# Layers A and B in turn on one core: masks of B built once, four row casts on ScalarE, eight homes for B's first tails

## The chip, the cores and the metric

The kernel runs on one core of one Trainium2 chip. The metric is the device time of one execution in microseconds (us), lower is better. The engines are TensorE (PE, with its weight loads as PEld), VectorE (DVE), ScalarE (ACT), GpSimd (POOL) and SyncE (SP, which here only issues DMAs). ScalarE issues some DMAs as well; its issues are shown as ACTq, those of SyncE as SPq.

## What is computed

Four layers, A, B, A, B, on 2048 rows of 640 numbers, each with a layer norm in front and a residual sum behind:

```python
x = A_x
x = x + _A_ref(_layernorm(x), A_wq, A_wk, A_wv, A_wo, A_beta)
x = x + _B_ref(_layernorm(x), B_mem0, B_Wq, B_Wk, B_Wv, B_Wo, B_seg_len)
x = x + _A_ref(_layernorm(x), ...)
x = x + _B_ref(_layernorm(x), ...)
```

A is attention with 32 heads of 20 over four segments of 512 rows; each segment also reads a running memory `M`, `z` of the segments before it. B is a recurrence over 64 steps of 32 rows; `mem` (8 rows, at first `mem0`) goes in front of each step's rows, and the first 8 rows of a step's result are the next step's `mem`:

```python
for s in range(n_seg):                       # 64 steps
    h = concat([mem, xs])                    # 8 + 32 rows
    q, k, v = h@Wq, h@Wk, h@Wv               # 32 heads of 128
    scores = where(mask, q@k.T * scale, -1e9)
    o = concat_heads(softmax(scores) @ v) @ Wo
    mem = o[:, :M]; outs.append(o[:, M:])
```

`mask` is the same in each step and in both B layers: keys of `mem` are open to everyone, the others are causal.

## The kernel before

`full_kernel` (line 1277) calls `layer_A` (line 217) and `layer_B` (line 728) in turn. B's `Wq` and `Wk` are resident in SBUF; `Wv` and `Wo` share their place with A's tiles and are loaded anew for each B layer. Rows pass from layer to layer through two DRAM tensors, `xres` (float32) and `xres_bf` (bfloat16).

**End of A.** A works through 4 segments by 8 head groups. The last work on a 128-row block is `out_stage_b` (line 330): ten `YP` matmuls in two halves, two DVE sums into `xnew`, a store of `xnew` to `xres` (line 346), a cast to bfloat16 into `xnb` (lines 347 and 348, on GpSimd) and a store of that to `xres_bf` (line 349). `xnb` is in a pool of one buffer, so each cast waits until the store before it has landed. The last segment has four such rows, numbered 0 to 3 here, and they are worked while B begins.

**B's lead-in** (lines 951 to 999) is all that stands ahead of B's first step. In the order in which it is written out:

- `ln_load`, `ln_norm`, `ln_spread` for four blocks of 128 rows: bfloat16 rows in, layer norm (its power on GpSimd), five transposes into a PSUM tile `b_lntps`, and two ScalarE copies, into `HX` and `TX`. `TX` holds the last 8 rows of each step ("tails").
- `init_masks` (line 770, called in line 960): `b_sel` and `b_mask12`, with two DVE sums, two DVE memsets, 16 selects on GpSimd over `b_maskf`, and two DVE casts.
- eight tail units, k = 0 to 7, four with `Wq` and four with `Wk`: 40 matmuls into a PSUM tile `b_tail`, then `tail_evac` (line 906): an evacuation into an SBUF tile `b_tu` (even k on ScalarE, odd k on DVE) and a DMA of 128 KB to DRAM `QKd` (line 913; even k issued by ScalarE, odd k by SyncE). The homes of `b_tu` are the ring `kq` of four buffers for k < 6, and two tiles of the `wk` pool for k = 6 and 7.
- four projections of 512 columns, `b_Kp`, `b_Qp`, `b_Kp`, `b_Qp`, evacuated into `b_kq` tiles of the same ring; then eight loads of `Wo`, 640 KB each (lines 718 and 719, on SyncE).
- transposes `b_TP` of these four, `init_state` (memsets), `tails_load` (line 875), which reads `QKd`.
- eight units `b_vtail` with `Wv`, each evacuated to a tile `b_vt` and stored in two halves to DRAM `VTd` (line 934; odd k issued by ScalarE, even k by SyncE). k = 6 and 7 use again the homes `vt` and `E0` of k = 0 and 1.
- two projections `b_V`, `vtails_in` (line 886), a first tail unit of the next eight steps; then step 0 begins with `b_Ka`.

B's instructions on each engine are kept in written order by a wrapper (line 106 is the wrapper's line, and so stands for most of B; line 135 does the same for A). Across the two layers a scheduler decides the order when the kernel is built. PSUM tiles of the lead-in (`b_lntps`, `b_tail`, `b_Kp`, `b_TP`, `b_vtail` and so on) come from one ring of five buffers. DMAs report by eight completion semaphores that are used in turn, so an issue can also wait for the landing of the DMA eight places before it.

**First A.** On GpSimd it begins with the zeros and pads of its tiles (`P.memset(NM...)`, `pads`) and then turns to `a_EK` and to casts of one element (line 709) that hold back loads of B's resident weights.

Of the kernel before, what the change touches and what calls it, by code (L numbers as in the profile page):

```python
# [18 lines left out]
F32 = mybir.dt.float32  # L19
BF16 = mybir.dt.bfloat16  # L20
ACT = mybir.ActivationFunctionType
ALU = mybir.AluOpType
# [15 lines left out]
def alloc_consts(tc, ctx):  # L38
    cp = ctx.enter_context(tc.tile_pool(name="consts", bufs=1))
    C = Consts()  # L40
    C.pool = cp
    C.identb = cp.tile([128, 128], BF16, name="c_identb")
    C.mhalf = cp.tile([128, 1], F32, name="c_mhalf")
    C.negu = cp.tile([128, 2, 128], BF16, name="c_negu")
    C.bdmask = cp.tile([128, 128], F32, name="c_bd")
    C.pad = cp.tile([128, 2, 12], BF16, name="c_pad")
    W = AWeights()
    W.g = cp.tile([128, 32], F32, name="a_g")
    W.omg = cp.tile([128, 32], F32, name="a_omg")
    return C, W  # L50

# [94 lines left out]
class KeyOrder:  # L146
# [14 lines left out]
    def close(self):  # L161
        for rows in self.rec.values():
            rows.sort(key=lambda r: r[:2])
            for a, b in zip(rows, rows[1:]):
                self.tc.add_manual_dep(b[2], a[2].name, self.info, reason="order")
        self.rec, self.base = {}, None


class AWeights:
# [9 lines left out]

def build_gates(nc, pool, W, A_beta):  # L180
    bb = pool.tile([128, 32], BF16, name="a_beta_bf")
    with nc.allow_non_contiguous_dma(reason="beta bcast"):
        nc.sync.dma_start(bb[:], A_beta.partition_broadcast(128))
    e = pool.tile([128, 32], F32, name="a_beta_e")
    nc.scalar.activation(out=e[:], in_=bb[:], func=ACT.Exp, scale=-1.0)
    nc.vector.tensor_scalar(out=e[:], in0=e[:], scalar1=1.0, scalar2=None, op0=ALU.add)
    nc.vector.reciprocal(out=W.g[:], in_=e[:])
    nc.vector.tensor_scalar(out=W.omg[:], in0=W.g[:], scalar1=-1.0, scalar2=1.0, op0=ALU.mult, op1=ALU.add)

# [27 lines left out]
def layer_A(nc, tc, C, W, x_src, x_dst, src_is_bf16, nseg=4, out_bf16=False, xb_dst=None, load_w=None, side_loads=None):  # L217
    SC = 1.0 / math.sqrt(20.0)
    nc_raw = nc
    nc = _OrdNC(tc, nc_raw, engines=("tensor",))  # L220
    K = KeyOrder(tc, nc_raw, A_LAGS)
# [3 lines left out]
    with ExitStack() as ctx:  # L225
        def pool(name, bufs):
            return ctx.enter_context(tc.tile_pool(name=name, bufs=bufs, reuse_waits="tile"))
# [12 lines left out]
        up = pool("a_unit", 3)  # L240
        wk = pool("a_wk", 2)
# [5 lines left out]
        st = pool("a_state", 1)  # L247
# [17 lines left out]
        def pads(i, eng):  # L265
            for on, dst, k in ((i < 2, Kn, 0), (True, vaug, 1)):
                if on:
                    src = C.pad[:, k, :].unsqueeze(1).unsqueeze(1).to_broadcast([128, 4, 4, 12])
                    (eng.copy if eng is nc.scalar else eng.tensor_copy)(dst[i][:, :, :, 20:32], src)
# [56 lines left out]
        def out_stage_b(n_, tt, halves=(0, 1)):  # L326
            d = SEG[n_]
            oT, xr = d["oT"][tt], d["xr"][tt]
            r0 = n_ * 512 + tt * 128
            if xr is None:  # L330
                xr = wkl.tile([128, D], BF16 if src_is_bf16 else F32, name="a_xr")
                nc.sync.dma_start(xr[:], x_src[r0:r0 + 128, :])
            if n_ == nseg - 1 and (tt or not src_is_bf16):
                d["xnew"] = up.tile([128, D], F32, name="a_xnew", tag="PT") if tt else xr
            elif 0 in halves:
                d["xnew"] = w1l.tile([128, D], F32, name="a_xnew") if src_is_bf16 else xr
            xnew = d["xnew"]
            for half in halves:
                YP = pg.tile([128, 320], F32, name="a_YP", tag="pg")
                for c in range(NCH):  # L340
                    nc.tensor.matmul(YP[:], lhsT=oT[:, c, :], rhs=W.wo[:, c, 320 * half:320 * half + 320],
                                     start=(c == 0), stop=(c == NCH - 1))
                K("xnew").vector.tensor_tensor(out=xnew[:, 320 * half:320 * half + 320], in0=YP[:], in1=xr[:, 320 * half:320 * half + 320], op=ALU.add)
            if 1 not in halves:
                return
            nc.sync.dma_start(x_dst[r0:r0 + 128, :], xnew[:])
            xnb = w1l.tile([128, D], BF16, name="a_xnb")
            K("xnb").gpsimd.tensor_copy(xnb[:], xnew[:])
            nc.sync.dma_start(xb_dst[r0:r0 + 128, :], xnb[:])

        GS = {}
# [220 lines left out]
        P = K("pads").gpsimd  # L572
# [4 lines left out]
                pads(1, P)  # L577
        pads(2, P)
        pads(3, P)
        K.base = None  # L580
        proj_q(0)
        proj_kv(0, 0)
# [67 lines left out]
        for g in range(NGR + 2):  # L650
            n, G = divmod(g, 8)
# [36 lines left out]
        for tt in range(4):  # L688
            out_stage_b(nseg - 1, tt)
# [38 lines left out]
def layer_B(nc, tc, C, W, x_src, xb_src, x_dst, mem0, B_Wv, B_Wo, nsteps=64, out_bf16=False, tag=""):  # L728
    SCB = 1.0 / math.sqrt(128.0)
    nc_raw = nc  # L730
    nc = _OrdNC(tc, nc_raw, engines=ORDER_ENGINES)
# [4 lines left out]
    with ExitStack() as ctx:  # L736
        def pool(name, bufs):
            return ctx.enter_context(tc.tile_pool(name=name, bufs=bufs, reuse_waits="tile"))
# [6 lines left out]
        kqp = pool("b_kqp", 4)  # L745
        W.wo = pool("b_wo", 1).tile([128, 32, D], BF16, name="b_wo")
        st = pool("b_state", 1)
        w2 = pool("b_w2", 2)
        wk = pool("b_wk", 1)
# [11 lines left out]

        Px = st.tile([128, 12, 32], BF16, name="b_Px")
        Pm = st.tile([128, 12, 32], BF16, name="b_Pm")
        mask12 = st.tile([128, 12, 40], BF16, name="b_mask12")
        QZ = [st.tile([128, 16, 24], BF16, name=f"b_QZ{i}") for i in range(2)]
        selm = st.tile([128, 2, 8], BF16, name="b_sel")
        HXz = st.tile([128, NCH, 1, 32], BF16, name="b_HXz")
        OTdef = [wk.tile([128, 32, 32], BF16, name=f"b_OTdef{i}") for i in range(2)]

        def init_masks():  # L770
            nc.vector.tensor_tensor(out=selm[:, 0, :], in0=C.identb[:, 24:32], in1=C.identb[:, 88:96], op=ALU.add)
            nc.vector.tensor_tensor(out=selm[:, 1, :], in0=C.identb[:, 56:64], in1=C.identb[:, 120:128], op=ALU.add)
            negs = wk.tile([128, 32], F32, name="b_negs", tag="PTa")
            nc.vector.memset(negs[:], -1e9)
            maskf = wk.tile([128, 2, 40], F32, name="b_maskf", tag="OTsb")
            nc.vector.memset(maskf[:], 0.0)

            def above(out, rows, ncol, base, chan, colstep=1):
                nc.gpsimd.affine_select(out=out, in_=negs[rows, 0:ncol], pattern=[[colstep, ncol]], compare_op=ALU.is_gt,
                                        fill=0.0, base=base, channel_multiplier=chan)  # L780

            for i in range(4):
                r8, r16, r32 = (slice(32 * i, 32 * i + w_) for w_ in (8, 16, 32))
                above(maskf[r16, 0, 0:8], r16, 8, 8, -1)
                above(maskf[r8, 0, 0:8], r8, 8, 0, -1)
                above(maskf[r32, 1, 8:32], r32, 24, 0, -1)
                above(maskf[r32, 1, 0:8], r32, 8, 24, -1, 0)
            nc.vector.tensor_copy(mask12[:, 0:4, :], maskf[:, 0, :].unsqueeze(1).to_broadcast([128, 4, 40]))
            nc.vector.tensor_copy(mask12[:, 4:12, :], maskf[:, 1, :].unsqueeze(1).to_broadcast([128, 8, 40]))

        def init_state():
            XO_ = bx.tile([64, 320], F32, name="b_XO", tag="XO")
# [9 lines left out]
        HX, TX, QT, KT, VH = {}, {}, {}, {}, {}  # L802
# [103 lines left out]
        def tail_evac(T, k, eng, home=None, dma=nc.sync.dma_start):  # L906
            proj, hg = divmod(k, 4)
            pool_, tg = home or (wk, "tu")
            tu = pool_.tile([128, 8, 8, 8], BF16, name="b_tu", tag=tg)
            evac(eng, tu[:].rearrange("p s h t -> p h s t"), tail_ps[0][:].rearrange("p h (s t) -> p h s t", t=8),  # L910
                 None if proj else SCB)
            o = 256 * proj + 64 * hg
            dma(QKd[8 * T:8 * T + 8, :, o:o + 64].rearrange("s p f -> p s f"), tu[:].rearrange("p s h t -> p s (h t)"))
# [42 lines left out]
        for g in range(n0):  # L956
            ln_norm(g)
            if g < 2:
                ln_spread(ln_ready.pop(0))
        init_masks()  # L960
        nc.gpsimd.memset(HX[0][:, :, 0, 0:8], 0.0)
        with nc.allow_non_contiguous_dma(reason="mem0 transpose load (tiny)"):
            for c in range(NCH):
                nc.sync.dma_start(HX[0][:, c, 1, 0:8], mem0[:, 128 * c:128 * c + 128].rearrange("t p -> p t"))
        for k in range(8):
            tail_unit(0, k, 0, 8, shared=True)
            tail_evac(0, k, "act" if k % 2 == 0 else "dve", (kqp, "kq") if k < 6 else (wk, ("tu", "OTsb")[k - 6]),
                      (nc.sync if k % 2 else nc.scalar).dma_start)
            if k in (1, 3) and ln_ready:
                ln_spread(ln_ready.pop(0))  # L970
# [81 lines left out]
        for s in range(nsteps):  # L1052
# [139 lines left out]
            PTa = wk.tile([128, 2, 4, 40], BF16, name="b_PTa", tag="PTa")  # L1192
# [12 lines left out]
            OTsb = wk.tile([128, 32 * 40], BF16, name="b_OTsb", tag="OTsb")  # L1205
# [161 lines left out]
```

## Time and profile before

| | us |
|---|---|
| three runs | 2710.68, 2709.66, 2705.59 (median 2709.66) |
| the profiled execution | 2707.02 |
| its span, first to last instruction | 2705.3 |
| first A | 0 to about 345 |
| first B: lead-in, then 64 steps | about 345 to 387, then to about 1340 |
| second A | to about 1693 |
| second B: lead-in, then 64 steps | about 1693 to 1736, then to the end |

In a row of a timeline stand the start, the duration, the engine, the line and operation, the tile written and the tiles read, and the count of instructions in the group; in brackets the idle time ahead of it and what ended that. A row with several instructions can have waits inside it. In the chain of waits a row is a start, a duration and the work (or the transfer) that the end waited for; "issue" is time in which the profile shows nothing to wait for. In a table of windows, PEclk is the granted TensorE clock as a share of full speed, and the DMA share is the mean busy share of the 16 DMA engines, which can be a little over 1. "Lead-in 1" and "lead-in 2" are those of the first and the second B; "the end of the lead-in" is the start of step 0's `b_Ka`.

### The profile page before, as it was taken

Reading aid. Unit: us, or ns where it says so; the run is one execution under the profiler, and the core shown is the slowest. Engines: PE = TensorE matmul, PEld = TensorE weight load, DVE = VectorE, ACT = ScalarE, POOL = GpSimd, SP = SyncE. Lnnn points to the kernel's source line nnn. Section 1 sums busy time; section 2 is a strip of 40 time slices with the busy share of each in tenths; the row PEclk is TensorE's granted clock in tenths of the full one; section 3 lists DMA queues with packets and bytes.
Section 4 is the critical chain, followed back from the end, with each engine's and each line's share of the span. In section 5 each row is a group of like instructions: output and inputs, shape, how many; then the busy total and the mean of one; then the engine's idle time right before and its main releaser. Section 6 shows DMA issues by size and latency. Waiting matters only on the chain.

```text
span 2705.3 us, 147013 instructions
## 1 busy us (share of the span) xinstructions
PE 2573.0 (95%) x65480; PEld 1697.2 (63%) x65480; DVE 1694.0 (63%) x4568; ACT 1578.6 (58%) x3712; POOL 717.1 (27%) x1651
## 2 busy tenths in 40 slices
PE   7999989999999999999989998899999999999998
PEld 4566556666666666666655565566666666666666
DVE  8999845555555555555589998355555555555555
ACT  6988935554555555554379888255555555555543
POOL 5677621111111111111146776111111111111110
PEclk9999999999999999999999999999999999999999
DMA  4122451222222222121220114511111121111110
GB/s 154 44 79 79 136 167 39 45 44 42 44 44 44 45 42 45 41 42 28 66 76 21 60 51 134 164 40 40 41 41 43 40 44 40 42 40 40 37 27 20
DMA packets 326620, 156.35 MB, mean 58 GB/s; under 512 B 246241, under 2 KB 310881, under 8 KB 324193
## 3 DMA queue, kind: packets, MB, share of 16 engines
q1 hardware_dynamic: 316384, 145.38, 21.3%
q8 instruction: 512, 8.39, 1.4%
q10 hardware_dynamic: 9600, 1.57, 0.3%
q14 instruction: 124, 1.01, 0.1%
HBM read 95.15 MB, written 51.71 MB: 54 GB/s over the span
## 4 chain that ended last, share of the span: by engine, by line
PE 79%; DVE 11%; ACT 5%; DMA 2%; issue 2%; POOL 1%; SPq 0%; ACTq 0%; DVEq 0%
PE b_OPS L106 11%; PE b_tail L106 6%; DVE a_nm L135 5%; PE b_Ka L106 5%; PE b_Qa L106 5%; PE b_Kb L106 5%; PE b_Qb L106 5%; PE b_Va L106 5%; PE b_Vb L106 5%; PE b_SP L106 4%; PE b_OTP L106 4%; PE b_vtail L106 3%; PE b_PTP L106 3%; PE b_OPSd L106 3%; ACT a_PT L135 3%; PE a_S L106 2%
## 5 line engine op out<-in xcount | busy, mean ns | idle before, releaser
L106 PEld LDWEIGHTS <-b_HX 128*32 128x32 bf16 x15360 | 431.8, 97 | 338.5 <-issue 11.9
L106 POOL TENSOR_TENSOR b_Pm<-b_E,b_rs 128x96 bf16<-128x96 bf16 x128 | 63.4, 496 | 1439.0 <-ACT b_Vth L106 1120.2
L135 DVE TENSOR_REDUCE a_nm<-a_S 128x2 f32<-128x512 f32 (+3 forms) x512 | 394.9, 815 | 30.6 <-PE a_S L106 22.4
L135 ACT ACTIVATE a_PT<-a_T 128x1024 bf16<-128x1024 f32 (+1 forms) x384 | 345.0, 903 | 26.8 <-PE a_T L106 18.2
L106 PE MATMUL b_OPS<-b_wo,b_OTsb 128*32 128x320 bf16 x8192 | 307.3, 300 | 9.7 <-issue 7.7
L106 PEld LDWEIGHTS <-b_OTsb 128*32 128x32 bf16 x8192 | 200.3, 96 | 95.3 <-DVE b_OTsb L106 24.7
L106 DVE CAST b_HX<-b_MT 128x8 bf16<-128x8 f32 x372 | 63.7, 172 | 278.1 <-PE b_MT L106 273.1
L135 POOL TENSOR_SCALAR_AFFINE_SELECT a_PT<-a_PT 128x256 bf16<-128x256 bf16 (+1 forms) x384 | 190.3, 505 | 125.6 <-ACT a_PT L135 124.5
L106 ACT CAST b_msb<-b_OPS 128x64 bf16<-128x64 f32 x378 | 69.4, 256 | 236.8 <-PE b_OPS L106 236.8
L106 ACT CAST b_kq<-b_Kb 128x512 bf16<-128x512 f32 x128 | 74.9, 585 | 202.6 <-PE b_Kb L106 202.6
L106 DVE COPY b_KT<-b_TPak 128x128 bf16<-128x128 bf16 x128 | 28.8, 225 | 226.7 <-PE b_TPak L106 226.7
L106 PEld LDWEIGHTS <-b_kq 128*128 128x128 bf16 x2080 | 117.0, 98 | 75.0 <-ACT b_kq L106 55.7
L106 PE MATMUL b_Ka<-b_wk,b_HX 128*32 128x512 bf16 x2520 | 160.8, 381 | 3.0 <-DVE b_vt L106 3.0
L106 DVE TENSOR_SCALAR b_kq<-b_Qa 128x512 bf16<-128x512 f32 x128 | 88.5, 692 | 116.2 <-PE b_Qa L106 113.3
L106 PE MATMUL b_Va<-b_wv,b_HX 128*32 128x512 bf16 x2520 | 160.8, 380 | 0.0
L106 PE MATMUL b_Qa<-b_wq,b_HX 128*32 128x512 bf16 x2520 | 160.1, 381 | 0.0
L106 PE MATMUL b_Vb<-b_wv,b_HX 128*32 128x512 bf16 x2520 | 160.1, 379 | 0.0
L106 PE MATMUL b_Kb<-b_wk,b_HX 128*32 128x512 bf16 x2520 | 159.2, 379 | 0.0
L106 PE MATMUL b_Qb<-b_wq,b_HX 128*32 128x512 bf16 x2520 | 159.0, 379 | 0.0
L106 DVE CAST b_OTsb<-b_OTP 128x160 bf16<-128x160 f32 (+1 forms) x384 | 122.6, 374 | 39.1 <-PE b_OTP L106 38.9
L106 PE MATMUL b_vtail<-b_wv,b_TX 128*32 128x256 bf16 x2880 | 141.2, 276 | 5.9 <-issue 4.1
L106 ACT ACTIVATE b_E<-b_SP 128x320 bf16<-128x320 f32 (+1 forms) x256 | 81.1, 368 | 109.9 <-PE b_Va L106 97.1
(202 smaller groups left out, 5772.7 us busy)
## 6 DMA issues: line engine op xcount, KB each, us to landing
b_tl<-b_QKd SPq DMA_DIRECT2D x128, 128.0 KB
b_QKd<-b_tu SPq DMA_DIRECT2D x120, 128.0 KB
b_wv<-in_B_Wv_dram SPq DMA_DIRECT2D x10, 1024.0 KB
b_wo<-in_B_Wo_dram SPq DMA_DIRECT2D x16, 640.0 KB
b_Vth<-b_VTd SPq DMA_DIRECT2D x512, 16.0 KB
b_VTd<-b_vt SPq DMA_DIRECT2D x240, 32.0 KB
b_XO<-xres SPq DMA_DIRECT2D x256, 30.0 KB
xres<-a_xnew SPq DMA_DIRECT2D x19, 320.0 KB
```

Source lines behind the costliest of these rows:

```text
L106: r = f(*a, **k)
L135: r = f(*a, **k)
```

## The change

1. `b_mask12` and `b_sel` become constants, `C.mask12` and `C.selm`. They are built once by a new function `build_masks`, all on GpSimd, in the first A layer behind the pads. `init_masks` and its call in B are gone.
2. In the last segment of each A layer the four `xnb` casts go to `nc.scalar.copy`, where before they were on GpSimd (and in A's sorted order of instructions, `K("xnb")`).
3. The tails k = 4 and 5 get homes of their own, `(w2, "QT")` and `(w2, "KT")`, so that of the ring `kq` only k = 0 to 3 are written by tails.

```diff
+    C.mask12 = cp.tile([128, 12, 40], BF16, name="b_mask12")
+    C.selm = cp.tile([128, 2, 8], BF16, name="b_sel")
...
+def build_masks(G, C, pool):
+    G.tensor_tensor(out=C.selm[:, 0, :], in0=C.identb[:, 24:32], in1=C.identb[:, 88:96], op=ALU.add)
+    G.tensor_tensor(out=C.selm[:, 1, :], in0=C.identb[:, 56:64], in1=C.identb[:, 120:128], op=ALU.add)
+    negs = pool.tile([128, 32], F32, name="b_negs", tag="am")
+    G.memset(negs[:], -1e9)
+    maskf = pool.tile([128, 2, 40], F32, name="b_maskf", tag="am")
+    G.memset(maskf[:], 0.0)
+
+    def above(out, rows, ncol, base, chan, colstep=1):
+        G.affine_select(out=out, in_=negs[rows, 0:ncol], pattern=[[colstep, ncol]], compare_op=ALU.is_gt,
+                        fill=0.0, base=base, channel_multiplier=chan)
+
+    for i in range(4):
+        r8, r16, r32 = (slice(32 * i, 32 * i + w_) for w_ in (8, 16, 32))
+        above(maskf[r16, 0, 0:8], r16, 8, 8, -1)
+        above(maskf[r8, 0, 0:8], r8, 8, 0, -1)
+        above(maskf[r32, 1, 8:32], r32, 24, 0, -1)
+        above(maskf[r32, 1, 0:8], r32, 8, 24, -1, 0)
+    G.tensor_copy(C.mask12[:, 0:4, :], maskf[:, 0, :].unsqueeze(1).to_broadcast([128, 4, 40]))
+    G.tensor_copy(C.mask12[:, 4:12, :], maskf[:, 1, :].unsqueeze(1).to_broadcast([128, 8, 40]))
...
-            K("xnb").gpsimd.tensor_copy(xnb[:], xnew[:])
+            if n_ == nseg - 1:
+                nc.scalar.copy(xnb[:], xnew[:])
+            else:
+                K("xnb").gpsimd.tensor_copy(xnb[:], xnew[:])
...
         pads(3, P)
+        if src_is_bf16:
+            build_masks(P, C, up)
...
-        mask12 = st.tile([128, 12, 40], BF16, name="b_mask12")
+        mask12, selm = C.mask12, C.selm
...
-        init_masks()
...
-            tail_evac(0, k, "act" if k % 2 == 0 else "dve", (kqp, "kq") if k < 6 else (wk, ("tu", "OTsb")[k - 6]),
+            tail_evac(0, k, "act" if k % 2 == 0 else "dve", (((kqp, "kq"),) * 4 + ((w2, "QT"), (w2, "KT"), (wk, "tu"), (wk, "OTsb")))[k],
```

(`src_is_bf16` is true for the first A layer alone.) Where the built program has these instructions:

- On ScalarE the four casts stand, after A's last copy of `oT`, as: cast 0, `HX`, `TX` of block 0, `HX` of block 1, cast 1, `TX` of block 1, casts 2 and 3; then the evacuation and the DMA of tail k = 0, `HX` and `TX` of block 2, the same of k = 2, `HX` and `TX` of block 3, and those of k = 4 and 6.
- On PE the ten `YP` matmuls of row 3 stand ahead of the first tail unit in lead-in 1 (before: behind 16 of its matmuls), and behind 52 tail matmuls in lead-in 2 (before: behind 60).
- On SyncE, in lead-in 1, the last `xres_bf` store is followed by the `QKd` store of k = 1, then `Wo` load 0, k = 3, load 1, k = 5, load 2, k = 7, loads 3 to 7; in lead-in 2 the order is as before (load 0, k = 1, k = 3, load 1, and so on). There the first `VTd` store now waits by its semaphore for `Wo` load 5, before for load 6.
- On DVE, in lead-in 2, both halves of `xnew` of rows 2 and 3 stand behind the layer norm's scaling of block 3.

More of the change, by code (lines that the diff above doesn't have):

```diff
@@ L763, in layer_B @@
         Pm = st.tile([128, 12, 32], BF16, name="b_Pm")
-        mask12 = st.tile([128, 12, 40], BF16, name="b_mask12")
+        mask12, selm = C.mask12, C.selm
         QZ = [st.tile([128, 16, 24], BF16, name=f"b_QZ{i}") for i in range(2)]
-        selm = st.tile([128, 2, 8], BF16, name="b_sel")
         HXz = st.tile([128, NCH, 1, 32], BF16, name="b_HXz")
         OTdef = [wk.tile([128, 32, 32], BF16, name=f"b_OTdef{i}") for i in range(2)]
[L770 to L789, printed above, removed]
         def init_state():
```

## The prediction

> **What bounds the kernel now.** I read the page first, for its span and the shares of its chain of waits:
>
> ```profile
> span 2705.3 us, 147013 instructions
> PE 79%; DVE 11%; ACT 5%; DMA 2%; issue 2%; POOL 1%; SPq 0%; ACTq 0%; DVEq 0%
> ```
>
> PE sets most of the end, but the change adds and removes no matmul. So only the stretches count in which PE waits. The chain's 2% of DMA are 54 us; the change can touch those that lie in the two lead-ins of B. PE's timeline there, first of lead-in 1, then of lead-in 2:
>
> ```profile
> 358.73 4.83 PE L106 MATMUL b_tail<-b_TX,b_wk 128*128 128x64 bf16 x160 [2.39 <-DVE b_tu L106]
> 368.48 2.33 PE L106 MATMUL b_Kp<-b_wk,b_HX 128*32 128x512 bf16 x20 [2.65 <-DVE b_tu L106]
> 374.80 4.55 PE L106 MATMUL b_vtail<-b_wv,b_TX 128*32 128x256 bf16 x160
> 386.91 2.15 PE L106 MATMUL b_Ka<-b_wk,b_HX 128*32 128x512 bf16 x20 [0.28 <-DVE b_vt L106]
> ...
> 1707.07 4.83 PE L106 MATMUL b_tail<-b_TX,b_wk 128*128 128x64 bf16 x160 [1.46 <-DVE b_tu L106]
> 1722.47 6.63 PE L106 MATMUL b_vtail<-b_wv,b_TX 128*32 128x256 bf16 x160
> 1736.43 1.79 PE L106 MATMUL b_Ka<-b_wk,b_HX 128*32 128x512 bf16 x20 [2.75 <-DVE b_vt L106]
> ```
>
> `b_Ka` is step 0; from there on nothing is changed. So what the change is worth is how much earlier the two `b_Ka` start. The chain of waits says what they wait for now. Lead-in 1:
>
> ```profile
> 359.75 0.73 POOL a_xnb L135
> ...
> 360.49 0.33 SPq L349
> ...
> 361.00 0.40 SPq L719
> ...
> 361.45 6.16 DMA b_QKd<-b_tu
> ...
> 367.73 0.70 DVE b_tu L106
> ...
> 368.45 5.14 DMA b_QKd<-b_tu
> ...
> 376.53 6.63 DMA b_VTd<-b_vt
> ...
> 383.18 3.13 DMA b_VTd<-b_vt
> ```
>
> Read it upwards: step 0 waits for a `b_vt` evacuation, that for a store to `VTd`, that for stores and evacuations behind `b_QKd`, and those, through SyncE, for the last row's cast on GpSimd at 359.75. Behind this cast's store (360.49) stands the first `Wo` load (361.00). The chain names small stores, but they take 5 to 7 us each. Three windows, two of lead-in 1 and one of lead-in 2, show why:
>
> ```profile
> 363.00:369.00 6.00, 3.35 (x68) 1.78 (x67) 1.27 (x3) 0.60 (x2) 0.00 (x0) 0.94 0.84 194
> 369.00:384.00 15.00, 12.63 (x296) 8.75 (x289) 3.44 (x9) 2.66 (x6) 0.00 (x0) 0.91 1.08 331
> 1711.00:1732.00 21.00, 16.40 (x349) 10.61 (x346) 4.20 (x9) 3.49 (x8) 0.00 (x0) 0.84 1.06 298
> ```
>
> The last two numbers are DMA share and GB/s: from 369 to 384 and from 1711 to 1732 the DMA engines are full, with eight loads of 640 KB. A small store stands among these loads and lands when they let it. So I take the end of each lead-in as the end of this stream.
>
> **The masks.** On GpSimd 16 selects and on DVE two casts go from each lead-in:
>
> ```profile
> 354.59 3.12 POOL L106 TENSOR_SCALAR_AFFINE_SELECT b_maskf<-b_negs 16x8 f32<-16x8 f32 x16 [0.88 <-PE b_lntps L106]
> 357.41 0.67 DVE L106 CAST b_mask<-b_maskf 128x160 bf16<-128x160 f32 x2 [2.94 <-POOL b_maskf L106]
> 358.01 1.27 DVE L106 TENSOR_SCALAR b_tu<-b_tail 128x512 bf16<-128x512 f32 x2
> ```
>
> The casts wait 2.94 us for the selects, and the evacuations of tails 1 and 3 wait behind them in DVE's order; PE's wait of 2.39 at 358.73 is that. The evacuations can now run when their tails are there, before 356. The four casts of rows no longer wait behind selects and memsets either, but that belongs to the next part.
>
> In the first A the same work is added to GpSimd:
>
> ```profile
> 18.87 0.45 POOL L135 TENSOR_SCALAR a_EK<-a_EK 128x320 f32<-128x320 f32 x1 [2.34 <-ACT a_EK L135]
> 19.32 0.18 POOL L709 COPY b_wk<-a_kT 1x1 bf16<-1x1 bf16 x1
> 25.33 0.18 POOL L709 COPY b_wq<-a_kT 1x1 bf16<-1x1 bf16 x1 [5.83 <-ACT a_kT L135]
> 27.18 0.48 DVE L135 SCALAR_TENSOR_TENSOR a_phik<-a_Kn,a_EK 128x320 bf16<-128x320 bf16 x1
> ```
>
> Selects 3.12, and I estimate 1.4 for two copies, two memsets and two sums (copies by the 0.72 that GpSimd takes for a cast of 640 columns, below): 4.5 us into idle stretches of 2.34 and 5.83. `a_EK` comes about 2.2 later, near 21, and DVE reads it first at 27.18. I cost it at nothing; this idle time is its cover, and without it the price is 2.2, at most 4.5. The load behind the cast at 19.32 also starts 2.2 later; it feeds B, 300 us on.
>
> **The casts on ScalarE.** Each cast waits for the landing of the store before:
>
> ```profile
> 352.49 0.72 POOL L135 CAST a_xnb<-a_xnew 128x640 bf16<-128x640 f32 x1 [2.31 <-DMA xres_bf<-a_xnb]
> ...
> 349.69 0.32 SPq L349 DMA_DIRECT2D xres_bf<-a_xnb  x1
> 353.23 0.32 SPq L349 DMA_DIRECT2D xres_bf<-a_xnb  x1
> ```
>
> From the store's issue at 349.69 to the next cast at 352.49 are 2.80. From 353.23 the last cast could then start at 356.0, where it now starts at 359.75. ScalarE's price of a cast is estimated from the 0.60 of `b_tu` below, 512 columns: 0.60 x 640/512 = 0.75, near GpSimd's 0.72. ScalarE is idle for 2.77 ahead of 352.32, so the casts find room; with 0.3 to 0.5 of order behind `HX` and `TX` copies I put the last store at 357.3 (now 360.49) and the first `Wo` load, 0.51 behind it as now, at 357.8: 3.2 earlier.
>
> The price is what is queued behind these casts on ScalarE, because there the fourth now stands ahead of tail 0:
>
> ```profile
> 352.32 0.60 ACT L106 ACTIVATE b_tu<-b_tail 128x512 bf16<-128x512 f32 x1 [2.77 <-PE b_tail L106]
> 352.95 0.39 ACTq L106 DMA_DIRECT2D b_QKd<-b_tu  x1
> 355.56 0.37 ACTq L106 DMA_DIRECT2D b_QKd<-b_tu  x1
> ...
> 355.90 0.44 PE L106 MATMUL b_lntps<-c_identb,b_xt 128*128 128x128 bf16 x5
> ```
>
> Tail 0's evacuation goes from 352.32 to about 356.8. Its PSUM buffer is the one that block 3's transposes take in a ring of five (two `lntps`, two tails, `lntps`, two tails, `lntps`), so these and the K tails behind them wait for it: K tails at 356.8 + 0.60 + 0.44 and 0.3 for issue, 358.1, against 358.73. The wait of 2.39 is thus taken over by ScalarE almost whole. And the two stores at 352.95 and 355.56, which are out ahead of the stream today, fall into it. Their price by the queue of ScalarE between 357 and 387:
>
> ```profile
> q10 hardware_dynamic: 3137, 0.53, 10.4%
> ```
>
> 10.4% of 30 us are 3.1, in which ScalarE issues two stores to `QKd` (128 KB each) and eight halves to `VTd` (32 KB each): half of the bytes each, so 0.8 for a store to `QKd`; at least 0 (it finds a gap), at most 3.1/2 = 1.55. I take 0.8 by the bytes, so 1.6 for two.
>
> Lead-in 2 has the same parts, on other times:
>
> ```profile
> 1701.86 0.72 POOL L135 CAST a_xnb<-a_xnew 128x640 bf16<-128x640 f32 x1 [1.05 <-DMA xres_bf<-a_xnb]
> 1707.55 0.72 POOL L135 CAST a_xnb<-a_xnew 128x640 bf16<-128x640 f32 x1
> 1708.80 0.39 SPq L719 DMA_DIRECT2D b_wo<-in_B_Wo_dram  x1
> ```
>
> The third cast must wait for `xnew`, which now stands behind a scaling on DVE: 1702.2. With 0.75 and the store's 2.8 the fourth starts at 1705.8, the first load at 1707.0, 1.8 earlier. K tails: 1705.8 + 0.75 + 0.60 + 0.44 = 1707.6 at the latest, against 1707.07, so nothing is to be gained there; the two stores fall into the stream as before.
>
> **The homes.** The second `Kp` waits 2.65 because its `kq` buffer is freed by a store of tail 4 or 5, which in the stream takes 6.16 and 5.14. With four tails on four buffers, `Kp` and `Qp` wait for tails 0 to 3 only, and those stores are issued before or at the head of the stream. K tails from 358.1 take 4.83, the projections 4 x 1.1 (four such lie between 386.91 and 391.04 + 1.26, the later ones 1.1 apart) end at 367.4, transposes and evacuations follow, and `b_vtail` starts at about 368.5, 6.3 earlier than 374.80; in lead-in 2 by the same steps from 1707.6 at about 1717.9, 4.6 earlier than 1722.47. By itself this ends nothing: the last `b_vt` wait for `VTd` stores, which wait for the loads.
>
> **The sum,** by the stream. Lead-in 1: it begins 3.2 earlier; two stores more cost 1.6; and `Kp`'s wait and SyncE's no longer thin it out at its head, where the window from 363 to 369 has 0.84 against 1.08, 6 x 0.24 = 1.4 us. So 3.2 - 1.6 + 1.4 = 3.0; bounds 3.2 - 3.1 = 0.1, if the stores cost most and the thin head stays, and 3.2 + 1.4 = 4.6. Lead-in 2: 1.8 - 1.6 = 0.2; the window there shows no thin head, but its first `VTd` store waits for load 5 in place of load 6, and one load is 0.655 MB / 298 GB/s = 2.2 us. The chain's last store stands behind that one on SyncE, so I take 2.0 of it: 2.2; bounds 1.8 - 3.1 = -1.3 and 1.8 + 2.2 = 4.0. Together 5.2, from -1.2 to 8.6.
>
> The profiled execution took 2707.02: 2701.8. It stands 2.6 under the median of the three runs, 2709.66, from which the sum gives 2704.5. I say **2702.5**, nearer to the first because one of the three runs, 2705.59, lies lower still.
>
> A rule speaks against a part of this. PE will now stand idle in one long piece, between `b_vtail`, which ends near 368.5 + 4.55 = 373 with two `b_V` behind it, and `b_Ka` near 384. The clock in such a place:
>
> ```profile
> 387.00:390.00 3.00, 3.00 (x44) 1.36 (x47) 0.45 (x1) 1.67 (x3) 0.00 (x0) 0.71 0.30 73
> 391.04 1.26 PE L106 MATMUL b_Qb<-b_wq,b_HX 128*32 128x512 bf16 x20
> ```
>
> Today the clock is 0.71 in the first 3 us of step 0, and `b_Ka` takes 2.15 where the fourth such projection takes 1.26: 0.89 lost. The Trainium skill, page "TensorE: Matmul & The Clock Gate", section "Part 1: The HAM clock gate", says that an idle window of some 3.4 us halves TensorE's clock and that as much busy time is needed to get it back. The trace agrees as far as it shows a lowered clock behind idle time; the rule would add up to 0.9 per lead-in if the whole of step 0's first 3 us went at half speed, and the sum by it is 5.2 - 1.8 = 3.4.
>
> **Rivals.**
>
> *PE's chain decides, not the stream.* If the `VTd` stores land soon after their issue, the earlier `b_vtail` is worth 6.3 + 4.6 = 10.9: 2696 from the profiled execution. For it: the chain runs through `b_vtail`. Against it: 6.63 for one small store in a window at 1.08. Chance 0.10.
>
> *The transfers hide it.* The stream is as full as it can be, and the loads that start earlier only push against stores that had the engines to themselves: gain 0 to 2.5, so about 1.2 and 2706. For it: both full windows are over 1; against it: 0.84 from 363 to 369. Chance 0.25.
>
> *Slower: ScalarE's order.* If the fourth cast starts later than about 358.1 (1705.9 in lead-in 2), 1.6 before its time now, the earlier stream no longer pays for the two stores. If it starts where it does now, 359.75, tail 0 is out at 361.1 and K tails start at 361.9, 3.2 late, and the two stores cost 1.6: +1.6 to +3.2 for each lead-in, some 5 for both, 2712. For it: ScalarE works in order, and in lead-in 2 the margin is 0.1. Against it: in lead-in 1 353.23 + 2.80 leaves 2 us. Chance 0.11. The clock's loss is inside the forecast's range.
>
> **How the numbers follow.** The forecast, a gain of 2.5 to 8.6, has 0.54. 0.2% are 5.4 us, about what a measurement of this kernel can tell. Since both executions' scatter and the sum's own 2 us lie around 5.2, of the forecast 0.35 lie beyond 5.4; of the first rival all, of the second 0.03: faster 0.48. Slower by over 5.4 is most of the third rival: 0.09. The rest, 0.43, is within. The range goes from the first rival, 2696, to the second at no gain against the median, 2709.5; the third lies outside.
>
> **What would show it.** Right: the first `Wo` load near 357.8 and 1707.0; tail 0's evacuation behind the last cast; no wait at the second `Kp`; `b_vtail` near 368.5 and 1717.9; a long idle stretch behind `b_V`, ended by `b_vt`, which waits for `VTd`; `b_Ka` near 383.9 and, less what lead-in 1 has gained (which goes off all times of lead-in 2 here), 1734.2. Wrong: `b_Ka` that follows `b_vtail` by less than 12 us (the first rival), a first load that isn't earlier (the third), or `a_phik` in the first A that waits for `a_EK` from GpSimd.

## The result, and the profile after

| | us |
|---|---|
| before, 8 runs | median 2710.99 (2705.59 to 2717.52) |
| changed, 8 runs | median 2703.65 (2700.74 to 2707.15) |
| ratio | 0.9976, 95% interval 0.9966 to 0.9985 |
| profiled execution of the changed kernel, and its span | 2705.0, 2703.2 |

By the ratio the change is worth 0.24%, 6.5 us of 2711 (4.1 to 9.2); the two medians lie 7.3 apart. The single runs of one kernel lie some 6 to 12 us apart, so I measure the lead-ins in the traces too. Their origin is the start of the first of the four last `xnb` casts, which in both kernels waits for nothing but DVE's sum. Timeline rows of these casts, before and after (the line numbers of the changed kernel are shifted: 106 is now 108, 135 is 137, 349 is 377, 719 is 749, 934 is 942):

```profile
345.31 0.72 POOL L135 CAST a_xnb<-a_xnew 128x640 bf16<-128x640 f32 x1 [0.95 <-DVE a_xnew L135]
1693.62 0.72 POOL L135 CAST a_xnb<-a_xr 128x640 bf16<-128x640 f32 x1 [1.82 <-DVE a_xr L135]
```

```profile
344.82 0.72 ACT L374 CAST a_xnb<-a_xnew 128x640 bf16<-128x640 f32 x1 [2.63 <-DVE a_xnew L137]
355.92 0.72 ACT L374 CAST a_xnb<-a_xnew 128x640 bf16<-128x640 f32 x1 [3.38 <-DMA xres_bf<-a_xnb]
356.56 0.59 ACT L108 ACTIVATE b_tu<-b_tail 128x512 bf16<-128x512 f32 x1
...
1694.08 0.72 ACT L374 CAST a_xnb<-a_xr 128x640 bf16<-128x640 f32 x1 [2.39 <-DVE a_xr L137]
1704.09 0.72 ACT L374 CAST a_xnb<-a_xnew 128x640 bf16<-128x640 f32 x1 [5.13 <-DVE a_xnew L137]
1707.10 0.72 ACT L374 CAST a_xnb<-a_xnew 128x640 bf16<-128x640 f32 x1 [2.29 <-DVE a_xnew L137]
```

PE's timeline of the changed kernel, both lead-ins:

```profile
357.47 4.83 PE L108 MATMUL b_tail<-b_TX,b_wk 128*128 128x64 bf16 x160
...
364.40 1.25 PE L108 MATMUL b_Kp<-b_wk,b_HX 128*32 128x512 bf16 x20
...
368.11 3.02 PE L108 MATMUL b_vtail<-b_wv,b_TX 128*32 128x256 bf16 x102
...
383.02 2.37 PE L108 MATMUL b_Ka<-b_wk,b_HX 128*32 128x512 bf16 x20
...
1703.67 2.83 PE L108 MATMUL a_YP<-a_wo,a_oT 128*128 128x320 bf16 x10 [2.48 <-DVE a_xnew L137]
...
1721.47 2.80 PE L108 MATMUL b_vtail<-b_wv,b_TX 128*32 128x256 bf16 x94
...
1735.82 1.52 PE L108 MATMUL b_Ka<-b_wk,b_HX 128*32 128x512 bf16 x12
```

No wait is left at the second `b_Kp` (2.65 before). Lead-in 1 takes 383.02 - 344.82 = 38.20 from its first cast to step 0, where it took 386.91 - 345.31 = 41.60: 3.4 less. Lead-in 2 takes 41.74, where it took 42.81: 1.1 less. Counted from the first cast, `b_vtail` starts 6.2 earlier in lead-in 1, but nearly half of that is lost again in waits behind it. SyncE shows where the two lead-ins part:

```profile
356.67 0.33 SPq L377 DMA_DIRECT2D xres_bf<-a_xnb  x1
...
357.68 0.62 SPq L749 DMA_DIRECT2D b_wo<-in_B_Wo_dram  x1
...
1707.81 1.37 SPq L1031 DMA_DIRECT2D b_XOd<-xres  x2
1709.23 0.55 SPq L377 DMA_DIRECT2D xres_bf<-a_xnb  x1
1709.96 1.64 SPq L749 DMA_DIRECT2D b_wo<-in_B_Wo_dram  x1
```

In lead-in 1 the first `Wo` load is issued 12.9 from the first cast (15.7 before). In lead-in 2 it is 15.9 (15.2 before): it has not come earlier at all. The first row of DVE below is of the kernel before, the rest, of DVE and GpSimd, of the changed one:

```profile
1700.87 0.44 DVE L106 TENSOR_SCALAR b_xt<-b_xt,b_ln_mv,b_ln_rstd 128x640 bf16<-128x640 bf16 x1
```

```profile
353.42 0.93 DVE L108 TENSOR_SCALAR b_xt<-b_xt,b_ln_mv,b_ln_rstd 128x640 bf16<-128x640 bf16 x1 [0.73 <-POOL b_ln_rstd L108]
1701.40 1.83 DVE L108 TENSOR_SCALAR b_xt<-b_xt,b_ln_mv,b_ln_rstd 128x640 bf16<-128x640 bf16 x1 [0.73 <-POOL b_ln_rstd L108]
1703.14 0.87 DVE L137 TENSOR_TENSOR a_xnew<-a_YP,a_xr 128x320 f32<-128x320 f32 x2
```

```profile
1701.31 0.13 POOL L108 MEMSET b_HX<- 128x40 bf16 x1
...
1702.81 0.23 POOL L108 MEMSET b_HXz<- 128x160 bf16 x1
```

With the selects gone, GpSimd's six memsets of the lead-in follow the last power at once and fall on DVE's scaling of block 3. In lead-in 2 it takes 1.83 in place of 0.44 and ends 0.2 behind the last memset; in lead-in 1 it takes 0.93. In lead-in 2 the `xnew` sums of rows 2 and 3 stand behind it, and behind those PE's last `YP` (2.48 of waiting), the third cast and the fourth.

The chain of waits in lead-in 2 of the changed kernel, up to step 0:

```profile
1723.59 8.83 DMA b_wo<-in_B_Wo_dram
...
1732.49 1.88 DMA b_VTd<-b_vt
1734.37 0.00 issue
1734.37 0.38 ACT b_vt L108
1734.75 0.04 issue
1734.80 1.26 PE b_vtail L108 x20
```

Here a `Wo` load stands in the chain itself: ScalarE's store of a `VTd` half is issued only when that load has landed (its semaphore is the load's). The next `b_vt` evacuation on ScalarE waits until the store has landed, 1.88 later, and then frees the PSUM buffer for the last `b_vtail`.

Outside the lead-ins the two kernels drift apart by 1 to 3 us where both have the same instructions: by the starts of `b_Ka` and `a_QP` the changed kernel's profile loses 1.5 in the first B's steps and 2.9 in the second A up to the first cast, its repetition (e0, below) wins 1.3 in the former and loses 1.0 in the latter. I put that down to scatter: from the last `b_Ka` to the fourth `a_QP` of the second A both profiles of the changed kernel take 1.8 more than the kernel before (48.56), but e7 (below), which is the kernel before but for four loads of B, takes 2.2 more. This scatter is why the lead-ins are compared by themselves.

### The profile page after: what moved, and what is told of

Its sections match the earlier page's. It is cut to its first block, busy times and chain, and to the rows that moved or that the text cites. A ratio compares the mean times of both kernels' runs of the same rounds, so it can differ in the third digit from the quotient of the medians.

```text
span 2703.2 us, 146987 instructions
## 1 busy us (share of the span) xinstructions
PE 2572.6 (95%) x65480; PEld 1695.3 (63%) x65480; DVE 1693.9 (63%) x4556; ACT 1583.5 (59%) x3720; POOL 709.4 (26%) x1633
## 5 line engine op out<-in xcount | busy, mean ns | idle before, releaser
L137 DVE TENSOR_REDUCE a_nm<-a_S 128x2 f32<-128x512 f32 (+3 forms) x512 | 394.9, 815 | 30.5 <-PE a_S L108 22.6
L108 PE MATMUL b_vtail<-b_wv,b_TX 128*32 128x256 bf16 x2880 | 139.3, 273 | 14.3 <-issue 8.6
```

Of the source, the lines that this page charges most:

```text
L108: r = f(*a, **k)
L137: r = f(*a, **k)
```

## The experiments

Each kernel was timed in rounds beside the kernel before (8 runs of the change, 5 of e11, 6 of e5, 11 or 12 of the others); the ratio is to that. The table has, for one profile of each, the distance from the first cast in us, lead-in 1 / lead-in 2. "Step 1" is step 1's `b_Ka`, so that what step 0 gives back is in it; "sum" adds step 1's two numbers.

| kernel | last cast | first `Wo` load | `b_vtail` | step 0 | step 1 | sum | ratio (95%) |
|---|---|---|---|---|---|---|---|
| before | 14.4 / 13.9 | 15.7 / 15.2 | 29.5 / 28.9 | 41.6 / 42.8 | 57.3 / 59.3 | 116.6 | |
| changed | 11.1 / 13.0 | 12.9 / 15.9 | 23.3 / 27.4 | 38.2 / 41.7 | 54.2 / 57.2 | 111.3 | 0.9976 (0.9966 to 0.9985) |
| changed again (e0) | 10.6 / 13.3 | 12.6 / 16.6 | 22.6 / 28.2 | 36.8 / 41.4 | 52.9 / 57.7 | 110.6 | 0.9977 (0.9966 to 0.9988) |
| e1, masks alone | 13.4 / 12.2 | 14.7 / 15.1 | 28.2 / 27.2 | 41.3 / 41.4 | 56.9 / 57.4 | 114.3 | 0.9981 (0.9969 to 0.9993) |
| e2, casts alone | 10.8 / 11.9 | 14.3 / 13.5 | 26.7 / 27.5 | 39.3 / 40.5 | 54.9 / 56.0 | 110.9 | 0.9981 (0.9969 to 0.9993) |
| e3, homes alone | 14.6 / 14.0 | 15.8 / 15.3 | 26.0 / 24.8 | 41.4 / 40.8 | 57.6 / 56.7 | 114.3 | 0.9996 (0.9985 to 1.0007) |
| e4, masks and homes | 11.3 / 13.2 | 12.6 / 15.3 | 23.5 / 26.0 | 38.0 / 41.3 | 55.0 / 58.5 | 113.4 | 0.9970 (0.9957 to 0.9984) |
| e5, memsets held | 10.9 / 11.7 | 13.1 / 15.0 | 22.9 / 26.4 | 37.5 / 40.4 | 53.9 / 56.5 | 110.3 | 0.9964 (0.9953 to 0.9976) |
| e10, e5 with GpSimd's casts | 13.1 / 11.7 | 14.3 / 13.0 | 22.6 / 23.2 | 39.7 / 37.7 | 56.1 / 54.3 | 110.4 | 0.9973 (0.9964 to 0.9982) |
| e6, changed, late loads | 12.0 / 13.2 | 13.7 / 16.6 | 25.0 / 27.5 | 37.5 / 41.4 | 55.3 / 59.2 | 114.4 | 0.9981 (0.9970 to 0.9993) |
| e7, before, late loads | 14.9 / 14.5 | 16.2 / 15.8 | 28.0 / 29.1 | 40.8 / 40.2 | 58.3 / 56.4 | 114.8 | 1.0003 (0.9995 to 1.0012) |
| e9, e5, loads tied late | 10.6 / 11.6 | 12.3 / 15.1 | 23.8 / 25.9 | 38.6 / 41.1 | 56.6 / 58.4 | 115.1 | 0.9990 (0.9978 to 1.0001) |
| e11, e9, and `b_tl` tied | 11.4 / 12.5 | 13.5 / 14.1 | 23.3 / 25.0 | 34.0 / 36.6 | 53.0 / 54.3 | 107.3 | 0.9947 (0.9934 to 0.9961) |
| e12, before with e11's ties | 14.9 / 15.0 | 16.2 / 16.3 | 29.2 / 29.9 | 38.5 / 40.8 | 57.8 / 56.4 | 114.2 | 0.9990 (0.9979 to 1.0002) |

**e0, the changed kernel again.**

> The changed kernel once more, for the scatter of one profile: from the first cast to step 0 it had 38.2 and 41.7 us. If these two repeat within 0.5, differences of 1 us between profiles mean something; if they move by 1 or more, only larger ones do. Time within 0.1% of 2703.65.

Step 0 moved by 1.4 in lead-in 1 and by 0.3 in lead-in 2, the sum by 0.7; the median, 2705.09, repeats within 0.1%. So a difference of less than about 1.5 us in one lead-in of one profile says nothing here.

**e1, e2, e3: one part alone.** e1 is the masks' part of the diff, e2 the `xnb` lines alone, e3 the line with the homes alone.

> Masks built in the first A as in the change; the four casts stay on GpSimd, the tails keep their old homes. Theory (the lead-in ends with the stream of Wo loads, and what starts the stream is the last row's cast): without the selects ahead of it the last cast starts near 356.5 in lead-in 1 (359.75 before), the first Wo load near 357.5 (361.00), the two ScalarE stores of QKd stay ahead of the stream, but the kq ring still thins it: step 0 3 us earlier in lead-in 1, 2 in lead-in 2, together 4 to 6 of the change's 6.5. Rival (the homes carry the gain, the stream does not follow its start): under 1.5 us together.

> Only the four casts go to ScalarE; masks are still built in each B, tails keep their homes. Theory: the last cast no longer stands behind the selects, the first load starts near 357.8 as in the change, but tail 0's evacuation is late and DVE's casts of the masks still hold tails 1 and 3; two stores fall into the stream: gain 0 to 3 us in all. Rival (the order on ScalarE costs more than the early start brings): 1 to 4 us slower than before.

> Only the homes of tails 4 and 5 change. Theory (stream): Kp's wait of 2.65 in lead-in 1 and the late Qp in lead-in 2 go, b_vtail starts 3 to 5 us earlier, but step 0 moves by under 1.5 us in each lead-in, since VTd stores still land with the loads: 0 to 2.5 us in all. Rival (PE's own chain decides): 5 to 8 us faster, nearly the whole of the change.

e1 came out smaller than expected in the trace: step 0 comes 0.3 and 1.4 earlier, the sum is 2.3 less than before. Its profiled execution, 2710.09, was the longest of its eleven; by the ratio e1 gains 5.1 (1.9 to 8.4), as expected. GpSimd's rows in e1, from which the expected early cast is missing, and DVE's beside them:

```profile
354.13 0.72 POOL L137 CAST a_xnb<-a_xnew 128x640 bf16<-128x640 f32 x1 [4.46 <-DMA xres_bf<-a_xnb]
354.81 0.55 POOL L108 TENSOR_TENSOR b_ln_rstd<-b_ln_rstd,c_mhalf 128x1 f32<-128x1 f32 x1
...
358.23 0.72 POOL L137 CAST a_xnb<-a_xnew 128x640 bf16<-128x640 f32 x1 [1.19 <-DMA xres_bf<-a_xnb]
```

```profile
355.39 1.83 DVE L108 TENSOR_SCALAR b_xt<-b_xt,b_ln_mv,b_ln_rstd 128x640 bf16<-128x640 bf16 x1 [2.59 <-POOL b_ln_rstd L108]
```

The third cast waits long for the store before it, block 3's power stands behind that cast, and the scaling meets the memsets again; in lead-in 1 the second `b_Kp` keeps its wait (2.64). e2 came out larger than expected: 5.7 in the sum, which is all that the whole change has. Its first load comes only 1.4 and 1.7 earlier, not 3.2 as expected for lead-in 1; there the store of tail 1 stands ahead of it on SyncE. Its casts no longer wait for the selects, and since the selects still hold the memsets back, its scalings take 0.45 in both lead-ins. e3 fits the stream: `b_vtail` starts 3.5 and 4.1 earlier, step 0 only 0.2 and 2.0, and the time isn't told from no change. The parts don't add (2.3 + 5.7 + 2.3 is 10.3, the change has 5.3 and 6.0 in two profiles; by the ratios, too, e1 and e2 have 5.1 each and the change 6.5): masks and casts free the same last cast, each in its own way.

**e4, the change without ScalarE's casts.**

> The change without its second part: the four casts stay on GpSimd, which has no selects left. Theory (the casts on ScalarE cost as much as they bring once the selects are gone): the first Wo load starts within 0.7 us of the change's 357.68 and 1709.96, tails 0 and 2 are stored ahead of the stream (QKd of tail 0 near 352.5 in place of 357.17), the stream is 1.6 us shorter: 1 to 3 us faster than the change. Rival (ScalarE's casts are a part that brings something): 1 to 3 us slower than the change, with a last cast later than 357 in lead-in 1.

The last cast lies where the change has it, within 0.3, and step 0 within 0.4. The rival (1 to 3 us slower) is not borne out, and what was expected (1 to 3 us faster) isn't either: tail 0's store, out 3 and 6 us earlier, buys nothing that these runs can show.

**e5 and e10, the memsets held.** One line ahead of them, in the changed kernel (e5) and in e4 (e10):

```diff
+        nc.gpsimd.tensor_copy(HX[0][0:1, 0, 0, 0:1], ln_xt[3][0:1, 0:1])
         nc.gpsimd.memset(HX[0][:, :, 0, 0:8], 0.0)
```

> The change, and GpSimd's memsets of the lead-in are held by a one-element copy that reads block 3's scaled rows, so that they run behind DVE's scaling. Theory (in the changed kernel the memsets, no longer behind selects, run beside that scaling and stretch it: 1.83 us in lead-in 2 and 0.93 in lead-in 1, 0.44 before): the scaling takes 0.44 to 0.46 in both, in lead-in 2 the xnew sums, the casts and the first Wo load come 1.2 to 1.6 earlier and step 0 0.5 to 1.5. Rival (the 1.83 has another cause, such as the bf16 rows still being written): it stays over 0.9.

> As e5_memsets_held, but the four casts stay on GpSimd (the change's second part undone). Theory (once the selects are gone and the memsets are out of the way, it is the same which engine casts): from the first cast to the first Wo load within 0.7 of e5's 13.1 and 15.0, to step 0 within 1 of 37.5 and 40.4; tail 0 stored 3 to 4 us earlier without use. Time within 0.1% of e5. Rival 1 (ScalarE's casts are what brings the gain): step 0 1.5 us or more later in each lead-in. Rival 2 (they cost, by the two stores that fall into the stream): 1.5 or more earlier.

Rows of DVE and GpSimd in e5:

```profile
1698.25 0.45 DVE L108 TENSOR_SCALAR b_xt<-b_xt,b_ln_mv,b_ln_rstd 128x640 bf16<-128x640 bf16 x1 [0.73 <-POOL b_ln_rstd L108]
```

```profile
1698.76 0.18 POOL L108 COPY b_HX<-b_xt 1x1 bf16<-1x1 bf16 x1 [0.55 <-DVE b_xt L108]
```

The scaling is back at 0.45 in both lead-ins and the last cast of lead-in 2 comes 1.4 earlier: the memsets were what stretched it. The first load of lead-in 2 comes only 0.9 earlier (1.2 to 1.6 were expected), since the two `b_XOd` loads still stand ahead of the last store. Step 0 of lead-in 2 comes 1.4 earlier than in the changed kernel, 1.0 earlier than in its repetition, which by itself is within the scatter. The median, 2701.26, is 3.8 below the 2705.09 of e0, run on the same chip, but the two intervals overlap, so a gain in time from holding the memsets is not shown. That DVE and GpSimd stand in each other's way here agrees with the Trainium skill, page "SBUF — State Buffer", section "Who interferes with whom", by which DVE in a 2-port mode contends with GpSimd for a port pair that they share, and the later of the two waits for the whole instruction of the other. The trace adds that DVE waited through a row of memsets, not one; in which mode the scaling ran, no run here shows. e10 moves the casts back to GpSimd: step 0 comes 2.2 later in lead-in 1 and 2.6 earlier in lead-in 2, where under 1 was expected of each, and why was not tried; the sum is that of e5 (110.4 and 110.3). Once the selects and the collision are gone, which engine casts makes no difference to the sum or the time that can be seen.

**e6, e7, e9, e11, e12: do the loads end the lead-in?** e6 and e7 move the calls for loads 4 to 7 behind `vtails_in(0)`, in the changed kernel and in the one before.

> The change with Wo loads 4 to 7 issued behind the VTd stores and the reads of V's tails, so after the start of step 0; only four loads lie in the lead-in. Theory (the lead-in ends with the stream): step 0 comes 3 to 6 us earlier in each lead-in than in the change (from the first cast 38.2 and 41.7 there), until PE's own chain (b_V's end, 30.6 from the first cast in lead-in 1) and a store of some 2.5 us bound it; some of it can be given back at step 0's b_OPS, which needs all of Wo. In all 4 to 10 us faster than the change. Rival (the end follows PE's chain and not the loads): step 0 within 1 us of the change.

> The kernel before with the same late loads 4 to 7 and nothing else. Theory (stream): step 0 comes 2 to 5 us earlier in each lead-in than before, since there too the last stores land with the loads. Then the stream bounds both kernels. Rival (before, the chain of tails, kq ring and b_vtail bounds the end as much): under 1 us.

These two didn't decide it: step 0 came 0.7 and 0.4 earlier in e6 and 0.8 and 2.6 in e7, mostly less than expected. SyncE's order isn't tied in B, and the scheduler put three of the four loads back among the `VTd` stores (in e6 at 28.4, 28.9 and 30.6 from the first cast, ahead of step 0 at 37.5). e9 ties them, on e5:

```diff
+        for k in range(4, 8):
+            tc.add_manual_dep(load_B_wo(nc, W, B_Wo, k).ins, vt_last[0, 6].ins.name, info, reason="order")
```

> As e5_memsets_held, but Wo loads 4 to 7 are tied behind the last VTd store that SyncE issues in the lead-in (the late loads of e6 and e7 had been put back among those stores, seven of eight still ahead of step 0). Theory (the lead-in ends when the stream of Wo loads lets the VTd stores land): with four loads fewer ahead, step 0 comes 3 to 6 us earlier than in e5 in each lead-in (from the first cast 37.5 and 40.4 there); the loads then run beside step 0, whose b_OPS, 12.7 us behind its start, needs all of Wo and may give 1 to 4 of it back. In all 2 to 8 us faster than e5. Rival (PE's chain and the VTd stores' own latency end the lead-in): step 0 within 1 us of e5's, and a time that is the same or, by the late loads, longer.

Step 0 didn't come earlier (1.1 and 0.7 later than in e5), which looked like the end of the theory. SyncE's timeline in e9 says why it wasn't tested yet:

```profile
371.34 4.68 SPq L883 DMA_DIRECT2D b_tl<-b_QKd  x2
376.11 0.79 SPq L1075 DMA_DIRECT2D b_XO<-xres  x1
376.96 1.17 SPq L942 DMA_DIRECT2D b_VTd<-b_vt  x2
...
383.47 2.93 SPq L749 DMA_DIRECT2D b_wo<-in_B_Wo_dram  x4
```

The scheduler had also pulled step 1's `b_tl` load ahead of the `VTd` stores. Its tile is the first one's, so it waits until that load has landed and GpSimd has copied it (3.0 and 1.0 us), and the first `VTd` store is issued at 32.5 from the first cast, as late as the loads had held it (377.51 - 344.82 = 32.7 in the changed kernel). e11 ties that load too:

```diff
+            if s == 1:
+                tc.add_manual_dep(r.ins, vt_last[0, 6].ins.name, ..., reason="order")
```

> As e9_wo_after_v, but the second b_tl load (step 1's tails), which stood ahead of the VTd stores on SyncE there and made them wait for GpSimd's copies of the first, is tied behind the last VTd store too, as it stands in the changed kernel. Theory (the lead-in ends with the landing of Wo loads, through stores and semaphores; in e9 SyncE's wait for the second b_tl had taken its place): with that wait gone too, the first VTd store is issued near 28 us from the first cast in lead-in 1 (32.5 in e9, 32.2 in the changed kernel) and step 0 starts 3 to 5 us earlier than in e5 (37.5 and 40.4 from the first cast); step 0's length gives back some 2 us, as in e9 (18.0 from its b_Ka to step 1's against 16.0). In all 2 to 6 us faster than e5. Rival (PE's chain, or the latency of stores and evacuations alone, ends the lead-in): step 0 within 1 us of e5's again.

SyncE, PE and two windows of e11, and a window of the changed kernel (the last two numbers of a window are DMA share and GB/s):

```profile
372.51 0.33 SPq L883 DMA_DIRECT2D b_tl<-b_QKd  x1
372.90 0.80 SPq L1077 DMA_DIRECT2D b_XO<-xres  x1
373.79 1.61 SPq L944 DMA_DIRECT2D b_VTd<-b_vt  x2
...
380.64 2.61 SPq L749 DMA_DIRECT2D b_wo<-in_B_Wo_dram  x4
```

```profile
374.20 2.43 PE L108 MATMUL b_V<-b_wv,b_HX 128*32 128x512 bf16 x40
377.41 1.33 PE L108 MATMUL b_tail<-b_TX,b_wq 128*128 128x64 bf16 x40 [0.79 <-ACT b_vt L108]
...
379.23 1.25 PE L108 MATMUL b_Ka<-b_wk,b_HX 128*32 128x512 bf16 x20
...
396.37 1.00 PE L108 MATMUL b_OPS<-b_wo,b_OTsb 128*32 128x320 bf16 x24 [1.41 <-issue]
```

```profile
370.00:380.00 10.00, 8.11 (x232) 6.89 (x224) 1.87 (x4) 1.35 (x4) 0.87 (x3) 1.00 0.51 141
384.00:388.00 4.00, 4.00 (x130) 2.67 (x125) 1.76 (x7) 2.79 (x6) 0.00 (x0) 1.00 1.07 381
```

```profile
369.00:382.00 13.00, 7.53 (x217) 6.54 (x206) 1.17 (x3) 1.49 (x4) 0.20 (x1) 0.88 0.93 305
```

The DMA engines are half idle where they were nearly full (0.51 against 0.93), the first `VTd` store goes out 28.6 from the first cast, and step 0 starts 3.5 and 3.8 earlier than in e5. `b_Ka` takes 1.25 there against 2.37 in e5; PE stands idle for 0.79 shortly ahead of it, in e5 for 1.79 and 2.86. The loads now fill the engines beside step 0, and PE has pauses there: 1.48 and 1.75 ahead of `b_Qa`, which waits for ScalarE's evacuation of `b_V`, and others that the profile lists as issue (1.41 in the middle of `b_OPS`). In the second step 0 the chain of waits names a late `Wo` load again (8.27), ahead of `b_OPS`. Of 7.3 us the two steps 0 give 4.3 back, and the sum is 3.0 less than in e5. Measured: 2696.9 (2693.9 to 2700.52), ratio 0.9947. It beats both kernels: its interval lies below those of the change and of its repetition. It overlaps e5's a little (0.9953 to 0.9976), so what the ties bring in time over e5 is seen only in the traces.

> The kernel before with Wo loads 4 to 7 and step 1's b_tl load tied behind the last VTd store, as in e11; nothing of the change. It asks whether the loads also ended the lead-in before the change, which the prediction's sum takes for granted. Theory (they did): from the first cast to step 0 at most 39.5 and 41 us, 41.6 and 42.8 in the kernel before. Since b_vtail still starts late here (29.5 and 28.9 from the first cast; it needs some 8 us more to b_V's end), less can be gained than e11's 3.5 and 3.8 over e5. Rival (before the change PE's chain through the tails and b_vtail ended it, or both did at once): within 1 us of 41.6 and 42.8. In all, with 2 us given back in each step 0: 0 to 3 us faster than before by the theory, 2 to 4 slower by the rival.

In the kernel before, the same ties bring step 0 3.1 and 2.0 earlier and the sum 2.4 down. `b_vtail`, 29 to 30 from the first cast, comes no earlier by more than 0.3. So the loads ended the lead-in there as well, with PE's chain close behind them. In time it is unclear (0.9990, up to 1.0002).

## Why the prediction was right

It said faster by 5.2 in the profile, 2702.5 in the median; measured were 4.5 (3.4 and 1.1) to step 0 in one profile and 6.2 in the other, 6.5 by the ratio, 2703.65. Which way the gain comes, by an earlier stream of loads, was right. That the sum came so near is partly luck: the stores' price, 1.6 a lead-in, doesn't show, and lead-in 2's first load came 2.5 later than forecast; these two errors point in opposite directions.

- **Masks in the first A cost nothing.** Confirmed: in the changed kernel GpSimd's rows are

```profile
16.47 3.09 POOL L137 TENSOR_SCALAR_AFFINE_SELECT b_maskf<-b_negs 16x8 f32<-16x8 f32 x16
...
20.31 0.45 POOL L137 TENSOR_SCALAR a_EK<-a_EK 128x320 f32<-128x320 f32 x1
```

  `a_EK` comes 1.4 later than before, not 2.2, and DVE reads it at 27.10 as ever.
- **Lead-in 1** (it began 0.5 earlier as a whole). The last cast at 355.92 (forecast 356.0), the first load at 357.68 (357.8), tail 0's evacuation at 356.56 (356.8), K tails at 357.47 (358.1), `b_vtail` at 368.11 (368.5). The gain, 3.0 forecast, was 3.4, and 4.8 in the second profile.
- **Lead-in 2.** The step that failed is "the fourth starts at 1705.8, the first load at 1707.0, 1.8 earlier". With the 0.46 by which the whole lead-in began later here taken off, the cast starts at 1706.6 and the load at 1709.5, 0.7 later than before. The term missing is the memsets: the prediction took their move ahead as freeing GpSimd and didn't ask what DVE does just then; 1.39 us (1.83 - 0.44) on the way to the casts, and e5 gets it back. Then the last `xres_bf` store stands behind two `b_XOd` loads on SyncE, 1.37 long: a queue that the prediction had not passed through; these two stand behind the store of the late `xnew`. `b_vtail` came 3.1 later than forecast. That 1.1 us were still gained, 2.2 forecast, fits the shorter distance to the end, 41.74 - 15.9 = 25.8 from first load to step 0 against 27.6; how much of that is the wait for load 5 in place of load 6 was not tried by itself.
- **The end is the stream of loads, not PE's chain.** Shown in the traces by e11 and e12, and by e3, where `b_vtail` came 3.5 to 4.1 earlier and step 0 much less. The way is not only bandwidth, as the prediction had it: the loads hold SyncE's and ScalarE's issues through the shared semaphores, and any other late wait in the same place (e9's `b_tl`) does as well.
- **The price of the two stores, 1.6 a lead-in,** doesn't show: e4 and e10, in which at least tail 0's store is out early, are no faster than the change and e5.
- **The clock.** In lead-in 1 step 0 starts at a lower clock than before, at less than the price of 0.9 that the prediction named. A window and a timeline row of the changed kernel:

```profile
383.00:386.00 3.00, 3.00 (x40) 1.33 (x32) 0.22 (x1) 1.65 (x3) 0.00 (x0) 0.53 0.38 96
```

```profile
385.15 1.60 PE L108 MATMUL b_Qa<-b_wq,b_HX 128*32 128x512 bf16 x20
```

  The granted clock is 0.53 against 0.71 before; `b_Ka` and `b_Qa` take 2.37 + 1.60 where they took 2.15 + 1.26, 0.56 more (0.72 in e0). In lead-in 2 it is not so: from the start of `b_Ka` to the end of `b_Qb` are 6.2 before, 5.3 in this profile and 6.2 in e0. A longer idle stretch of PE thus came with a lower clock in one lead-in of the two.

Of the rivals, PE's chain and the slower one fell. The point from which the latter was to decide, the fourth cast less than 1.6 earlier, was reached in lead-in 2, where it is 0.9 earlier, and yet step 0 was no later. That the transfers hide it holds for the homes alone; the whole change, 4.1 to 9.2 by its interval, lies above that rival's 0 to 2.5.

## What to carry to other kernels

Take work off an engine and the work behind it moves up: look at what it then runs beside, as the memsets here ran beside a fast DVE operation. Before you shorten a chain, ask whether large loads that nobody needs yet stand among its small stores; moving these loads and one early `b_tl` load behind what waits, with the memsets held, gave as much again as the whole change. And when an experiment that takes a wait away changes nothing, look in its trace for the next wait in the same place before you drop the theory.

## What was not expected of the hardware

A scaling of 128x640 on DVE took 1.83 us in place of 0.44 while GpSimd ran six memsets in a row (1.73 in all), and ended just behind the last. It did so in lead-in 2 of the changed kernel, of its repetition and of e6, and in both lead-ins of e1 and e4 (1.79 to 1.83). In lead-in 1 of the first three it took 0.93 and ended while the row was still running. It stayed at 0.43 to 0.45 wherever the memsets came later (e2, e3, e5, e7 and e9 to e12). One cast of GpSimd is enough: in e1, e4, e7, e10 and e12 a scaling of block 1 that began 0.06 to 0.09 behind a row's cast of 0.72 took 0.81 to 0.84 and ended 0.17 to 0.18 behind that cast. And DMAs that share a completion semaphore in turn tie an issue on ScalarE to a load of SyncE's eight places before: the chain of the changed kernel has such a load with 8.83 us in it.
